# A one-core transform, gated block and expert kernel: VectorE's long steps cut up, column products put off, list scatters one at a time

## The chip, the cores and the metric

The kernel runs on one core of one Trainium2 chip. The metric is the device time of one execution in microseconds (us), the median of several runs. The engines are named as the profile names them: PE is TensorE's matmuls, DVE is VectorE, ACT is ScalarE, POOL is GpSimd and SP is SyncE, which issues most of the transfers.

## What is computed

There are three layers over 8 sequences of 3072 tokens with 256 channels, all in float32. The core of the reference:

```python
X = np.fft.rfft(x, axis=1)
Yr = shrink(Xr @ w_r - Xi @ w_i + b_r); Yi = shrink(Xr @ w_i + Xi @ w_r + b_i)   # soft threshold, 0.01
x = np.fft.irfft(Yr + 1j * Yi, n=3072, axis=1).reshape(24576, 256)
x = (sigmoid(x @ w_gate) * (x @ w_val)) @ w_out                                  # 256 -> 1536 -> 256
e = argmax(x @ moe2_gate); g = softmax(x @ moe2_gate)[e]                         # 8 experts
out = x + (x @ w_skip > 0) * g * (relu(x @ w1[e]) @ w2[e])                       # 256 -> 1024 -> 256
```

## The kernel before

To keep float32 accuracy on a float16 array, a matrix is stored as a high half and a low half, and each product is three matmuls (high-high, high-low, low-high). The high half comes from ACT and the low half from a subtraction on DVE or POOL, so every product waits for an ACT and then a DVE or POOL instruction. The power-of-two scale of a tile is the largest magnitude over all partitions; the maximum over partitions is a small matmul ("spread", line 188) that rides in a bank of the gated block.

**The main loop.** The gated block is 768 units: 8 batches of 8 chunks (384 tokens) of 12 slices of the 1536 channels (`moe_gen`, line 969). A unit u issues 12 matmuls of 384 columns for gate and value of its own slice (line 986), then 9 matmuls of 265 columns for the slice of unit u-2 (line 1028). Between the two lie, for each slice, a sigmoid on ACT (tile `sg`), the product of gate and value on DVE (tile `h`), the high half on ACT and the low half on DVE (both in tile `hh`). In DVE's program the low half of unit u comes after everything that was queued behind unit u's product.

**The background.** After each unit, `build` runs steps of five other jobs, written as Python generators whose `yield` ends a step: `attn` (the forward transform, mixing and half of the inverse of the next batch, `attn_gen`, line 496), `y` (the rest of the inverse, one chunk of 384 tokens at a time), `route` (expert choice and lists for a finished batch, `route`, line 1066), `prep` (expert weights) and `start`. The order of the instructions on each engine is the order in which the steps were issued, so the planner, not the hardware, decides what stands in front of what. A step's cost is estimated by a `Meter` (line 141): 0.07 us for each instruction plus its elements at the engine's rate; the cost of a step is the larger of VectorE plus GpSimd and ScalarE. A unit has room for 2.0 us (`BUDGET`), of which up to 0.3 (`CARRY`) is carried over; overdrawn room is carried as well. Jobs have due times in units, and of those that are due the one that is longest due goes first. `attn` is spread over a stretch of units in proportion to its steps' costs; `k.due` puts a single step off without moving that plan, so later steps run closer together until the plan is met. `route` has a step each 3.2 units (1.0 in the last batch). When `y` is due for a batch that `attn` has not finished (a few units after its planned end), it runs the rest of `attn` itself, and these steps count against no room.

**The places that the change touches.**

- Chunks of the forward transform (lines 656 to 676). Step by step for chunk c: load the input of chunk c+3 (SP); `cols`, 24 matmuls of 256 columns, and `evict`; `amax`; then settle the scale of chunk c+1 and write its high half on ACT (1024 elements), whose low half on DVE is put off to the head of the next step; then two steps that bound chunk c+3.
- Scales of a batch (lines 690 to 722). One step: the maximum over the batch comes back from its spread, ten operations on single columns follow, then the bias tile `bb` (five operations of 256 or 512 elements) and `bg` (512 elements). Four steps of 0.5 us (`WAITS`) that issue nothing follow before the first `freq`.
- Frequency groups (`freq`, `mix_pair`, `inv`; 13 groups a batch). The group's sum tile `sm` is split on POOL (tile `x`), ACT reuses the buffer for `com`, and POOL then adds `bg` to it (`yf`), on the way to the second mixing product.
- Routing's second step (lines 1086 to 1096): eleven DVE operations, on 192 elements for a whole batch (T = 24 tiles of 128 tokens) and on 24 for a chunk of the last batch (T = 3).
- The scatter of routed entries (lines 1126 to 1133): T indirect DMAs issued by POOL, three to a step.

Of the kernel before, what the change touches and what calls it, by code (L numbers as in the profile page):

```python
# [9 lines left out]
F32 = mybir.dt.float32  # L10
# [3 lines left out]
ALU = mybir.AluOpType  # L14
AX = mybir.AxisListType

NB, SEQ, D = 8, 3072, 256
N1, N2, NK, HN = 48, 64, 24, 32
NJ = 4
NC = HN // NJ  # L20
CT = 2 * N1 * NJ
NT3 = CT // 128
# [10 lines left out]
WAITS = 4  # L33
# [107 lines left out]
class Meter:  # L141
# [5 lines left out]
    def __getattr__(self, name):  # L147
        f = getattr(self.eng, name)

        def call(*a, **kw):  # L150
            self.sum += 0.07 + max(v.free_size() for v in a if hasattr(v, "free_size")) / self.rate
            return f(*a, **kw)  # L152

        return call
# [53 lines left out]
def absmax(k, out, in_, axis=AX.X):  # L208
    k.V.tensor_reduce(out, in_, axis=axis, op=ALU.max, apply_absolute_value=True)
# [286 lines left out]
def attn_gen(k, b):  # L496
    nc, V = k.nc, k.V
# [20 lines left out]
    def load(i):  # L518

        e, c = b + i // NC, i % NC  # L520
        if e < NB:
            xv = k.d.x[e].rearrange("(n h j) d -> h n j d", h=2, j=HN)
            x32[e, c] = k.xbuf[c % 4 if e == 0 else (e * NC + c) % 3]
            for h in range(2):
                nc.sync.dma_start(x32[e, c][h * 64:h * 64 + N1], xv[h, :, c * NJ:(c + 1) * NJ, :])

    def bound(c, h=None):
        if h is None:
            absmax(k, mx[:, 0, c:c + 1], x32[b, c], axis=AX.XY)
        else:  # L530
            absmax(k, (px if h else mx)[:, h, c:c + 1], x32[b, c][:, 2 * h:2 * h + 2], axis=AX.XY)
        if h == 1:
            V.tensor_tensor(mx[:, 0, c:c + 1], mx[:, 0, c:c + 1], px[:, 1, c:c + 1], op=ALU.max)
        if h == 1:
            tops[c] = allpow(k, px[:, 0, c:c + 1], mx[:, 0, c:c + 1], 2.0**-40)

    def scale(c):
        yield from settle(k, tops.pop(c))
        inv_pow2(k, px[:, 1, c:c + 1], px[:, 0, c:c + 1], 9)
# [35 lines left out]
    def amax(c):  # L575
        a_ = ah.pop(c).rearrange("p h j l e -> p (h j) l e")
        absmax(k, px[:, 2, c:c + 1], a_[:, :, 0], axis=AX.XY)
# [60 lines left out]
    if b == 0:  # L638
        for c in range(4):
            load(c)  # L640
        k.pace = 0.0
        yield
        k.pace = R1
        yield from first_cols()
    else:
        bg = k.gp.tile([128, 2, D], F32, tag="bg", name=f"bg_{b}", bufs=1)
        yield
        for c in range(3):
            bound(c, 0)
            yield  # L650
            bound(c, 1)
            yield
        yield from scale(0)
        halve(0)
        yield
        for c in range(NC):
            load(c + 3)
            yield
            cols(c, ((k.pa, "pa"),) * 2)
            evict(c, 0)  # L660
            evict(c, 1)
            yield
            if c > 0:
                amax(c - 1)
            yield
            if c + 1 < NC:
                yield from scale(c + 1)
                halve(c + 1)
            else:
                scales()  # L670
            yield
            if c + 3 < NC:
                bound(c + 3, 0)
                yield
                bound(c + 3, 1)
                yield
        yield 0.5
        amax(NC - 1)
    V.tensor_tensor(px[:, 2], px[:, 2], px[:, 0], op=ALU.mult)
    V.tensor_reduce(col(0), px[:, 2], axis=AX.X, op=ALU.max)  # L680
    top = allpow(k, col(3), col(0), 2.0**-60)
# [3 lines left out]
    def fetch(g):  # L685
        al = als[g] = k.wp.tile([128, 2, 2, D], F16, tag="al", name=f"al_{b}_{g}", bufs=AL)
        for i, k1 in enumerate(groups[g]):
            src = asc.rearrange("(r q) j l e -> q j r (l e)", r=4)[k1]
            nc.sync.dma_start(al[:, i].rearrange("p l e -> p (l e)"), src)

    for g in range(AL):
        fetch(g)
    yield
    if b:
        yield from settle(k, top)
    inv_pow2(k, col(4), col(3), 1)
# [4 lines left out]
    V.scalar_tensor_tensor(col(8), col(5), 2.0**-29, col(7), op0=ALU.mult, op1=ALU.mult)  # L701
    V.tensor_scalar(col(9), col(7), LAM, None, op0=ALU.mult)
    V.tensor_scalar(col(10), col(7), -LAM, None, op0=ALU.mult)
    bb = k.sp.tile([128, 2, D], F32, tag="bb", name=f"bb_{b}", bufs=1)
    for i in range(2):
        V.tensor_scalar(bb[:, i], k.bias[:, 0], k.chk[:, NC + i:NC + i + 1], None, op0=ALU.mult)
        V.scalar_tensor_tensor(
            bb[:, i], k.bias[:, 1], k.chk[:, NC + 2 + i:NC + 3 + i], bb[:, i], op0=ALU.mult, op1=ALU.add
        )
    if b:  # L710
        V.tensor_scalar(bb, bb, col(7), None, op0=ALU.mult)
    else:
        V.tensor_scalar(bb, bb, col(7), col(9), op0=ALU.mult, op1=ALU.add)
# [7 lines left out]
        V.tensor_scalar(col(14), col(10), 2.0, None, op0=ALU.mult)  # L721
    yield
    k.pace = 1.0
    for _ in range(WAITS):
        V.sum += 0.5
        yield

# [338 lines left out]
def route(k, b, t0, T):  # L1066

    nc, V, rp = k.nc, k.V, k.rp
    R = k.R[b][:, t0:t0 + T]
    L, S = R[:, :, 1:], R[:, :, 0]  # L1070
    tile_ = lambda tag, dt=F32, shape=None: rp.tile(shape or [128, T * NE], dt, tag=tag, name=f"{tag}_{b}_{t0}", bufs=1)
    tt = tile_("rt", shape=[128, 4, T])
    mx, sm, ac, gt = (tt[:, i] for i in range(4))
    et = lambda v: v.rearrange("p (e t) -> p e t", e=NE)
    te = lambda v: v.rearrange("p (e t) -> p t e", e=NE)
    bc = lambda v: v.unsqueeze(1).broadcast_to([128, NE, T])
    be = lambda v: v.unsqueeze(2).broadcast_to([128, NE, T])
    Le = L.rearrange("p t e -> p e t")
    dl, oh, w1, w2 = tile_("rdl"), tile_("roh"), tile_("rw1"), tile_("rw2")
    V.tensor_reduce(mx, L, axis=AX.X, op=ALU.max)  # L1080
    V.tensor_tensor(et(dl), Le, bc(mx), op=ALU.subtract)
    V.tensor_scalar(w1, dl, 0.0, None, op0=ALU.is_ge)
    k.S.activation(w2, dl, AF.Sigmoid)
    k.S.activation(dl, dl, AF.Sigmoid, scale=-1.0)
    yield
    V.reciprocal(dl, dl)
    V.tensor_tensor(dl, w2, dl, op=ALU.mult)
    V.tensor_tensor(et(w1), et(w1), be(k.rc[:, 0:NE]), op=ALU.mult)
    V.tensor_reduce(mx, te(w1), axis=AX.X, op=ALU.max)
    V.tensor_tensor(et(oh), et(w1), bc(mx), op=ALU.is_equal)  # L1090
    V.tensor_reduce(sm, te(dl), axis=AX.X, op=ALU.add)
    V.tensor_scalar(sm, sm, 1e-9, None, op0=ALU.add)
    V.reciprocal(gt, sm)
    V.tensor_scalar(ac, S, 0.0, None, op0=ALU.is_gt)
    oa = tile_("roa", F16)
    V.tensor_tensor(et(oa), et(oh), bc(ac), op=ALU.mult)
    yield
    ps = k.pa.tile([128, 512], F32, tag="pa", name="ps")
    W = T * NE
    nc.tensor.matmul(ps[:, :W], k.m16[:, 0], oa, start=True, stop=True)  # L1100
    nc.tensor.matmul(ps[:, W:2 * W], k.m16[:, 1], oa, start=True, stop=True)
    tot = tile_("rtot")
    V.tensor_copy(tot, ps[:, W:2 * W])
    V.tensor_tensor(w1, ps[:, :W], tot, op=ALU.subtract)
    yield
    V.memset(w2, 1.0)
    V.memset(et(w2)[:, :, 0:1], 0.0)
    V.tensor_tensor(et(tot)[:, :, 0], et(tot)[:, :, 0], k.base, op=ALU.add)
    inc = tile_("rdl")
    V.tensor_tensor_scan(inc, w2, tot, 0.0, op0=ALU.mult, op1=ALU.add)  # L1110
    V.tensor_copy(k.base, et(inc)[:, :, T - 1])
    yield
    V.tensor_tensor(w1, w1, inc, op=ALU.add)
    V.tensor_tensor(et(w1), et(w1), be(k.rc[:, NE:2 * NE]), op=ALU.add)
    V.tensor_tensor(w1, w1, oa, op=ALU.mult)
    V.tensor_reduce(sm, te(w1), axis=AX.X, op=ALU.add)
    yield
    V.tensor_scalar(ac, ac, -BIG, BIG, op0=ALU.mult, op1=ALU.add)
    idx = rp.tile([128, T], I32, tag="ridx", name="ridx", bufs=2)
    V.tensor_tensor(idx, sm, ac, op=ALU.add)  # L1120
    ent = rp.tile([128, T, 4], F32, tag="rent", name="rent", bufs=2)
    V.memset(ent[:, :, 3:4], 0.0)
    V.tensor_copy(ent[:, :, 0], gt)
    V.tensor_scalar(ent[:, :, 1:3], k.ids[:, t0:t0 + T, :], float(b * SEQ), None, op0=ALU.add)
    yield
    for t in range(T):
        if t % 3 == 0 and t:
            yield
        nc.gpsimd.indirect_dma_start(  # L1129
            out=k.lst, out_offset=bass.IndirectOffsetOnAxis(ap=idx[:, t:t + 1], axis=0),  # L1130
            in_=ent[:, t, :], in_offset=None, bounds_check=LROWS * BT - 1, oob_is_err=False,
        )
    yield
# [251 lines left out]

def build(tc, d, nb=NB, nstat=NSTAT, dbg=None):
    PSTEP = 3.9 * nb / NB
    BUDGET = 2.0
    CARRY = 0.3
    LEAD = 9  # L1390
    YSTEP = 0.9
    PRE = 2
# [9 lines left out]
    k = K()  # L1402
# [5 lines left out]
    with ExitStack() as top, tc.manual_schedule():  # L1408
# [166 lines left out]
        for _ in moe_gen(k, [(b, c) for b in range(nb) for c in range(NC)]):  # L1575
            room = min(room, CARRY) + BUDGET
            while room > 0:
# [94 lines left out]
```

## Time and profile before

| what | us |
|---|---|
| median of 3 runs (3607.19 to 3609.6) | 3607.56 |
| the profiled execution, its own time | 3600.82 |
| its span, first to last instruction | 3598.9 |

The profiled execution has a mean granted TensorE clock of 0.983. A line of a profile view names the line of the kernel, the engine, the operation and the tiles (out <- in). Where a helper records the operations, they all have line 152, and the tiles tell them apart. "Idle before" is the time for which the engine stood still before an instruction, and the name behind the arrow is what ended the wait. PEclk is the granted share of the clock: 1.0 is 2.4 GHz and 0.5 is 1.2 GHz.

### The profile page before, as it was taken

The page shows a single profiled execution, that of the slowest core. Times are in us where ns is not written, and L with a number is a line of the kernel's source. Part 1 is how long each engine was busy: PE and PEld are TensorE (multiplying, and loading weights), DVE is VectorE, ACT ScalarE, POOL GpSimd, SP SyncE. Part 2 cuts the span into 40 slices and gives each one's busy share as a digit, 9 for nine tenths or more (in the row PEclk, how much of TensorE's full clock was granted, in tenths as well). Part 3 has the DMA queues.
Part 4 walks back from the last instruction along what each step waited for, and adds up shares of the span by engine and source line. Part 5 has one row for each costly group of instructions (what it writes and reads, how often), then busy time and mean ns, then how long its engine had stood idle before and what let it go on. Part 6 is the DMA issues. An engine that isn't in the chain of part 4 may idle for free. (4 is left out here: it accounts for less than half of the span.)

```text
span 3598.9 us, 69199 instructions
## 1 busy us (share of the span) xinstructions
PE 3384.8 (94%) x26957; PEld 2379.7 (66%) x26958; DVE 2352.7 (65%) x5505; ACT 1664.2 (46%) x3276; POOL 698.3 (19%) x677
## 2 busy tenths in 40 slices
PE   4679999999999999999999999999999999999997
PEld 3456766676677666666766676667766666667675
DVE  7867677667776766666667676767645555665554
ACT  4545455455554544454445454544443343333332
POOL 3500100220031002200220022002200211333332
PEclk9889999999999999999999999999999999999999
DMA  6334233323322323232223231322211021444442
GB/s 167 116 101 120 75 96 93 90 70 97 103 82 75 110 72 89 69 97 86 81 72 96 80 102 57 97 75 81 84 42 37 28 86 51 149 145 144 163 155 102
DMA packets 230330, 336.07 MB, mean 93 GB/s; under 512 B 40705, under 2 KB 184835, under 8 KB 222736
## 3 DMA queue, kind: packets, MB, share of 16 engines
q1 hardware_dynamic: 213824, 305.31, 28.1%
q0 software_dynamic: 15744, 25.99, 2.4%
q8 instruction: 212, 3.47, 0.4%
q14 instruction: 118, 0.97, 0.1%
q10 hardware_dynamic: 432, 0.33, 0.0%
HBM read 177.86 MB, written 134.09 MB: 87 GB/s over the span
## 5 line engine op out<-in xcount | busy, mean ns | idle before, releaser
L986 PE MATMUL pg<-yT,wgv 128*128 128x384 f16 x9216 | 1654.7, 328 | 16.6 <-ACT sg L152 12.9
L986 PEld LDWEIGHTS <-wgv 128*128 128x128 f16 x9216 | 886.6, 98 | 565.8 <-issue 58.7
L1028 PE MATMUL pz<-wo,hh 128*128 128x265 f16 x6912 | 922.6, 278 | 26.8 <-DVE hh L152 22.7
L152 DVE TENSOR_TENSOR hh<-h,hh 128x384 f16<-128x384 f32 x768 | 447.8, 583 | 623.8 <-ACT hh L152 622.1
L1028 PEld LDWEIGHTS <-hh 128*128 128x128 f16 x6912 | 675.4, 98 | 225.6 <-DVE hh L152 31.3
L152 ACT ACTIVATE sg<-pg,ys 128x384 f32<-128x384 f32 x768 | 442.9, 577 | 570.8 <-PE pg L986 569.6
L152 DVE SCALAR_TENSOR_TENSOR h<-pg,sg 128x384 f32<-128x384 f32 x768 | 422.7, 550 | 5.3 <-PE pg L986 5.3
L152 ACT CAST hh<-h 128x384 f16<-128x384 f32 x768 | 387.0, 504 | 60.9 <-DVE h L152 60.6
L1129 POOL DMA_INDIRECT lst<-rent,ridx x192 | 197.1, 1027 | 573.7 <-DVE rent L152 310.2
L1374 PE MATMUL py<-we,h 128*128 128x256 f16 x2400 | 271.4, 273 | 1.4 <-DVE h L152 0.7
L1354 PE MATMUL ph<-zT,we 128*128 128x512 f16 (+3 forms) x1344 | 267.1, 356 | 5.6 <-DVE h L152 4.8
L152 POOL TENSOR_TENSOR ah<-tmp,ah 128x512 f16<-128x512 f32 x64 | 74.1, 1157 | 938.9 <-ACT ah L152 665.4
L1374 PEld LDWEIGHTS <-h 128*128 128x128 f16 x2400 | 233.3, 98 | 33.7 <-DVE h L152 1.6
L1354 PEld LDWEIGHTS <-we 128*128 128x128 f16 x1344 | 127.7, 98 | 135.4 <-issue 10.4
L152 POOL TENSOR_TENSOR x<-sm,x 128x256 f16<-128x256 f32 x77 | 56.1, 729 | 817.7 <-ACT x L152 614.7
L152 PEld LDWEIGHTS <-x 128*128 128x128 f16 x1842 | 182.2, 100 | 37.8 <-DVE sm L152 5.4
L152 ACT ACTIVATE h<-ph 128x512 f16<-128x512 f32 (+3 forms) x224 | 122.2, 548 | 183.7 <-PE ph L1354 181.5
L152 DVE SCALAR_TENSOR_TENSOR h<-ph,h 128x512 f16<-128x512 f32 (+3 forms) x224 | 141.1, 632 | 62.4 <-ACT h L152 60.8
L1380 POOL DMA_INDIRECT out_dram<-og,ix x100 | 99.4, 994 | 247.8 <-DVE gr L152 82.8
L152 DVE SCALAR_TENSOR_TENSOR og<-py,gr,zg 128x256 f32<-128x256 f32 x100 | 48.3, 483 | 141.6 <-PE py L1374 141.1
L1310 POOL DMA_INDIRECT zg<-zs,ix x100 | 102.3, 1023 | 131.3 <-DVE zh L152 38.4
L152 PE MATMUL ps<-wri,x 128*128 128x256 f16 x918 | 123.2, 281 | 4.5 <-ACT y L152 2.0
(236 smaller groups left out, 3391.1 us busy)
## 6 DMA issues: line engine op xcount, KB each, us to landing
we<-w SPq DMA_DIRECT2D x56, 1024.0 KB, 5.4
x<-in_x_dram SPq DMA_DIRECT2D x128, 192.0 KB, 3.5
asc<-ah SPq DMA_DIRECT2D x256, 96.0 KB, 2.0
al<-asc SPq DMA_DIRECT2D x192, 128.0 KB, 2.6
zsc<-zh SPq DMA_DIRECT2D x192, 128.0 KB, 2.1
zt<-zsc SPq DMA_DIRECT2D x64, 384.0 KB, 3.9
zs<-zo SPq DMA_DIRECT2D x64, 384.0 KB, 2.6
yh<-yn SPq DMA_DIRECT2D x308, 64.0 KB, 2.0
```

The source lines that it names most:

```text
L152: return f(*a, **kw)
L986: nc.tensor.matmul(ps[:, :CT], k.wgv[:, t, g, a, f * 128:(f + 1) * 128], yT[:, t, w, :], start=n == 0, stop=n == 5)
L1028: nc.tensor.matmul(zs[(b, c)][t][:, :ZW], hh[:, a, t * 128:(t + 1) * 128], k.wo[:, f, w, :], start=f == 0 and i == 0, stop=f == NF - 1 and ...
L1129: nc.gpsimd.indirect_dma_start(out=k.lst, out_offset=bass.IndirectOffsetOnAxis(ap=idx[:, t:t + 1], axis=0), in_=ent[:, t, :], in_offset=No ...
L1310: nc.gpsimd.indirect_dma_start(out=st.z[:, q, :], out_offset=None, in_=zs, in_offset=bass.IndirectOffsetOnAxis(ap=st.ix[:, 1, q:q + 1], ax ...
L1354: k.nc.tensor.matmul(ps, st.w[0][:, a, t * FE + f * 128:t * FE + (f + 1) * 128], st.zT[:, t, w, :], start=m == 0, stop=m == 5,)
L1374: k.nc.tensor.matmul(ps[:, :D], st.h[f][:, a, q * 128:(q + 1) * 128], st.w[1][:, w, f * D:(f + 1) * D], start=n == 0, stop=n == 23,)
L1380: k.nc.gpsimd.indirect_dma_start(out=k.d.out, out_offset=bass.IndirectOffsetOnAxis(ap=st.ix[:, 0, q:q + 1], axis=0), in_=o[:, q], in_offse ...
```

## The change

The meter charges 0.15 us for an instruction instead of 0.07, and a unit has room for 2.5 us with 0.4 carried instead of 2.0 with 0.3. In `attn_gen`, for all batches but the first, the step with a chunk's products may run no earlier than two units after the step that queued the chunk's low half. The last `amax` of a batch gets a step of its own; the bias tile is written ahead of the settling of the batch's scale, in two steps; the column operations are one step and the scaled bias tiles another; one empty step follows instead of four. Routing's second step is three steps where T is over 3. Scatters go one to a step in batches 0 to 5 and stay at three to a step in the last two.

```diff
@@ Meter
-            self.sum += 0.07 + max(v.free_size() for v in a if hasattr(v, "free_size")) / self.rate
+            self.sum += 0.15 + max(v.free_size() for v in a if hasattr(v, "free_size")) / self.rate
@@ attn_gen, chunks of batches 1 to 7
         for c in range(NC):
             load(c + 3)
+            k.due = k.unit + 2
             yield
             cols(c, ((k.pa, "pa"),) * 2)
             evict(c, 0)
...
         yield 0.5
         amax(NC - 1)
+        yield
     V.tensor_tensor(px[:, 2], px[:, 2], px[:, 0], op=ALU.mult)
...
     for g in range(AL):
         fetch(g)
     yield
+    bb = k.sp.tile([128, 2, D], F32, tag="bb", name=f"bb_{b}", bufs=1)
+    for i in range(2):
+        V.tensor_scalar(bb[:, i], k.bias[:, 0], k.chk[:, NC + i:NC + i + 1], None, op0=ALU.mult)
+        V.scalar_tensor_tensor(
+            bb[:, i], k.bias[:, 1], k.chk[:, NC + 2 + i:NC + 3 + i], bb[:, i], op0=ALU.mult, op1=ALU.add
+        )
+        if b:
+            yield
     if b:
         yield from settle(k, top)
     inv_pow2(k, col(4), col(3), 1)
...
     V.tensor_scalar(col(10), col(7), -LAM, None, op0=ALU.mult)
-    bb = k.sp.tile([128, 2, D], F32, tag="bb", name=f"bb_{b}", bufs=1)
-    for i in range(2):
-        V.tensor_scalar(bb[:, i], k.bias[:, 0], k.chk[:, NC + i:NC + i + 1], None, op0=ALU.mult)
-        V.scalar_tensor_tensor(
-            bb[:, i], k.bias[:, 1], k.chk[:, NC + 2 + i:NC + 3 + i], bb[:, i], op0=ALU.mult, op1=ALU.add
-        )
     if b:
+        yield
         V.tensor_scalar(bb, bb, col(7), None, op0=ALU.mult)
...
     k.pace = 1.0
-    for _ in range(WAITS):
+    for _ in range(1 if b else WAITS):
         V.sum += 0.5
         yield
@@ route
     V.reciprocal(dl, dl)
+    if T > NT3:
+        yield
     V.tensor_tensor(dl, w2, dl, op=ALU.mult)
     V.tensor_tensor(et(w1), et(w1), be(k.rc[:, 0:NE]), op=ALU.mult)
     V.tensor_reduce(mx, te(w1), axis=AX.X, op=ALU.max)
+    if T > NT3:
+        yield
     V.tensor_tensor(et(oh), et(w1), bc(mx), op=ALU.is_equal)
...
     for t in range(T):
-        if t % 3 == 0 and t:
+        if t and (b < NB - 2 or t % NT3 == 0):
             yield
         nc.gpsimd.indirect_dma_start(
@@ build
-    BUDGET = 2.0
-    CARRY = 0.3
+    BUDGET = 2.5
+    CARRY = 0.4
```

## Rows read from the trace of the kernel before

**Rows 1.** The page, part 1: busy time, share of the span, instructions.

```profile
PE 3384.8 (94%) x26957; PEld 2379.7 (66%) x26958; DVE 2352.7 (65%) x5505; ACT 1664.2 (46%) x3276; POOL 698.3 (19%) x677
```

**Rows 2.** Busy time in the main loop: length, engines, PEclk, DMA share, GB/s.

```profile
200.00:3020.00 2820.00, 2728.21 (x21965) 1915.61 (x21964) 1883.20 (x4388) 1375.06 (x2741) 419.60 (x404) 0.99 0.28 80
```

**Rows 3.** PE's waits from 200 to 3020: us in total, times, longest.

```profile
PE pz L1028 <- DVE hh L152: 22.7, 18, 2.2
PE ps L152 <- DVE xh L152: 20.7, 17, 3.1
PE pg L986 <- ACT sg L152: 12.9, 11, 3.7
...
PE ps L152 <- ACT xh L152: 4.6, 5, 1.6
```

**Rows 4.** Timeline, one inverse, one chunk's products: start, us, engine, instruction, [idle before].

```profile
820.74 0.38 PE L152 MATMUL ps<-yh,f 128*128 128x512 f16 x1 [2.83 <-DMA yh<-yn]
...
1273.03 1.15 ACT L152 ACTIVATE xh<-x,px 128x1024 f16<-128x1024 f32 x1 [2.85 <-DVE px L152]
...
1276.22 1.28 DVE L152 SCALAR_TENSOR_TENSOR xh<-x,px,xh 128x1024 f16<-128x1024 f32 x1
1277.55 1.28 PE L152 MATMUL ps<-xh,c 48*64 48x256 f16 x20 [3.01 <-DVE xh L152]
```

**Rows 5.** Stretches behind long waits of PE, columns as in rows 2.

```profile
1276.00:1284.00 8.00, 6.45 (x40) 3.68 (x40) 3.89 (x12) 3.21 (x6) 1.16 (x1) 0.57 0.37 98
...
2385.00:2390.00 5.00, 5.00 (x24) 2.93 (x25) 3.09 (x6) 2.12 (x4) 0.00 (x0) 0.66 0.16 52
...
1819.00:1824.00 5.00, 5.00 (x24) 2.64 (x22) 4.68 (x9) 2.43 (x6) 2.19 (x3) 0.66 0.17 55
...
820.00:825.00 5.00, 4.26 (x29) 2.86 (x30) 1.72 (x3) 1.69 (x4) 0.00 (x0) 1.00 0.74 248
```

**Rows 6.** Timeline at the scales of batch 2 (first line) and of batch 7.

```profile
640.07 0.40 PE L1028 MATMUL pz<-wo,hh 128*128 128x265 f16 x2 [1.44 <-DVE hh L152]
...
2379.16 0.55 DVE L152 SCALAR_TENSOR_TENSOR h<-pg,sg 128x384 f32<-128x384 f32 x1
...
2380.75 0.15 DVE L152 TENSOR_SCALAR bs<-bs 128x1 int32<-128x1 int32 x1
...
2384.38 0.55 DVE L152 TENSOR_TENSOR hh<-h,hh 128x384 f16<-128x384 f32 x1
...
2384.99 0.63 PE L1028 MATMUL pz<-wo,hh 128*128 128x265 f16 x4 [2.05 <-DVE hh L152]
```

**Rows 7.** Timeline at routing's second step, batches 0, 3 and 6.

```profile
609.74 0.40 PE L1028 MATMUL pz<-wo,hh 128*128 128x265 f16 x2 [1.26 <-DVE hh L152]
...
1692.84 1.34 DVE L152 RECIPROCAL rdl<-rdl 128x192 f32<-128x192 f32 x1
...
1698.20 0.36 DVE L152 TENSOR_TENSOR roa<-roh,rt 128x192 f16<-128x192 f32 x1
...
2754.02 0.29 PE L1028 MATMUL pz<-wo,hh 128*128 128x265 f16 x1 [2.24 <-DVE hh L152]
```

**Rows 8.** Timeline at scatters in front of a frequency group, three places.

```profile
690.49 0.48 PE L986 MATMUL pg<-yT,wgv 128*128 128x384 f16 x1 [2.80 <-ACT sg L152]
...
1815.52 0.97 POOL L1129 DMA_INDIRECT lst<-rent,ridx  x1 [1.37 <-DMA lst<-rent,ridx]
...
1817.23 0.47 ACT L152 ACTIVATE com<-ps,bs 128x256 f32<-128x256 f32 x1 [7.29 <-POOL x L152]
...
1818.22 1.14 PE L986 MATMUL pg<-yT,wgv 128*128 128x384 f16 x6 [3.73 <-ACT sg L152]
...
2179.21 0.32 PE L986 MATMUL pg<-yT,wgv 128*128 128x384 f16 x1 [1.25 <-ACT sg L152]
```

**Rows 9.** The products of batches 1 and 3: count, ns min/median/max, first and last start.

```profile
L152 PE MATMUL ps<-xh,c x192: 266/269/294, 225.5 to 309.4; 48*64 48x256 f16 x192
...
L152 PE MATMUL ps<-xh,c x192: 266/269/293, 845.8 to 944.8; 48*64 48x256 f16 x192
```

## The prediction

> **What bounds the kernel now.** I read the page's engine shares first: PE is busy for 94% of the span, VectorE for 65%, nothing else comes near [rows 1]. So a microsecond is won only where PE stands still or runs at the low clock. The second view cuts the span: in the main loop, 200 to 3020 us, PE is busy for 2728 of 2820 us, and the mean granted clock is 0.99 [rows 2]. That leaves 92 us of standing still, and about 28 us of clock (0.01 of 2820). The third view says what ended the waits of that stretch [rows 3]: low halves of the gated block (`hh`) 22.7 us in 18 waits, low halves of the transform's input (`xh`) 20.7 us in 17 and their high halves 4.6 us in 5, sigmoids (`sg`) 12.9 us in 11. Then I looked at the timeline where the long ones lie, and at the clock behind them. The unit's length is 2820 / 768 = 3.67 us.
>
> The start (to 200 us) and the expert blocks (from 3020 us) hold nothing that the change moves much: batch 0 keeps its steps apart from the bias tile's place, and T = 3 in the last batch's routing. I take both as unchanged.
>
> **The products behind the halves.** At 1273.03 ACT writes a chunk's high half, 1.15 us. VectorE's low half stands at the head of the next step and starts at 1276.22, behind the gated block's work, for 1.28 us. PE has the 24 matmuls in its program by then and waits 3.01 us for it [rows 4]. With two units, 7.3 us, between the step that queues the low half and the products, both have long ended: all of 20.7 + 4.6 = 25.3 us goes [rows 3]. Five of these waits have a fall of the clock to 1.2 GHz behind them, two of them like the one from 1276 with 0.57 over 8 us, three with 0.66 over 5 us, as the other falls are [rows 5]. Half rate for 0.86 of 8 us, some 6.9 us, of which 1 us was the wait itself, costs 3 us; half rate for 0.68 of 5 us, 3.4 us, costs at most 1.7, less the wait's tail 1.5. Together 2 x 3 + 3 x 1.5 = 10 us. **Term: -35.**
>
> What the wait delays: evictions, `amax` and the next chunk's scale come after it in the same generator; nothing else of the five jobs waits, and on the engines nothing stands in a queue, because the wait is in the planner. The load of chunk c+3 keeps its place ahead of it on SP. The price is lateness. The chunks of batch 1 lie (309.4 - 225.5) / 7 = 12 us or 3.3 units apart, those of batch 3 14.1 us or 3.9 units [rows 9]. Two units now pass idle for `attn`; the rest of a chunk needs about two more (the low half alone 1.28 us, and as much again for `amax` and the two bounds, which are as many elements). So batch 1 falls behind by 0.7 of a unit a chunk, five to six units in eight chunks, the others by almost nothing. Its frequency groups have the larger room to catch up; what is not caught up is run by `y` in a heap. Bounds: 0 if it catches up, 15 us if three groups are run one behind the other with PE standing for their chains. I take **+5**, nearer to 0, as the new room is a quarter larger.
>
> **A batch's scales.** In batch 7, VectorE has from 2380.75 to 2384.38, 3.6 us, of column operations and bias tiles ahead of the low half that PE wants; PE waits 2.05 us [rows 6]. From the end of the gated product (2379.71) to that low half 4.67 us pass, and the wait is 2.05, so some 2.6 us of background behind one product cost nothing. The new pieces are 0.8 us (one bias tile), again 0.8, about 1.5 (columns) and 1.3 us; any one fits, and two as well. Six of the 18 waits for `hh` stand behind this step, 1.44 the first and 2.05 the last, 9.9 us by my count. Three have a clock fall behind them like that of batch 7 from 2385 [rows 5], 1.7 us each. 9.9 + 5.1. **Term: -15.** The bias tile moves ahead of the settling of the scale; only the first and last frequency group of a batch read it, ten units later, and the last reader of the batch before is done. No instruction is added; the empty steps that go are paid by the new steps' own spacing.
>
> **Routing's second step.** From 1692.84 to 1698.56 VectorE works for it, 5.7 us, some of it held up by POOL's operations. Six of the 18 waits stand behind this step, 1.26 the first and 2.24 the last [rows 7], 9.4 us by my count, three with a clock fall. The pieces are 1.3, 1.3 and 1.9 us and lie 3.2 units apart. 9.4 + 5.1. **Term: -14.** The chunk-wise routing of the last batch keeps its step.
>
> **Scatters.** A scatter takes 0.97 us of POOL and waits for the landing of the one before, 1.37 us, so three hold POOL for over 7 us; ACT's `com` waits 7.29 us behind them, the sigmoid behind it on ACT, and PE 3.73 us for that [rows 8]. Three such places: 2.80 + 3.73 + 1.25 = 7.8 us; two clock falls add 2.6. A single scatter finds its forerunner landed, and holds `com` for 1 us. The place with a hold of 7.29 cost 3.73, so some 3.5 us are free. **Term: -10.** The work stays 192 scatters, but a batch's list takes 24 steps of 3.2 units instead of 8, with the other steps just over the 96 units of a batch; the lists of batches 1 to 5 so start late by some units each, and catch up in the last batch, where steps come each unit. The expert tables are needed only near unit 732, so I cost it at nothing; the cover is those units.
>
> **Meter and room.** The meter's 0.15 us is what a single-column operation takes [rows 6]. Costs of a 512-element step rise by an eighth, of small ones by double, the room by a quarter: a unit may get more, up to 2.9 us and the last step's overhang. That is over the 2.6 us that cost nothing. Six short waits for `hh`, 3.4 us in all, already come from such heaps. Bounds: -3 if they go, +45 if one unit in ten gets 0.6 us too much. I take **+10**, nearer to the row.
>
> **Sum.** -35 - 15 - 14 - 10 + 5 + 10 = -59 against the profiled execution's own 3600.8 us: 3542. The median of the runs shown is 6.7 us above that execution, so I forecast 3548 for a median.
>
> **The clock, row and rule.** The clock's part of the sum is 10 + 5 + 5 + 2.6 = 23 us. The rows tie falls to these waits: 0.66 from 2385, behind the wait of 2.05 us at 2384.99, yet 1.00 at 820, around a wait of 2.83 us [rows 4 to 6]. So a wait of two or three microseconds may cost the clock or not. The Trainium skill, page "TensorE: Matmul & The Clock Gate", Part 1, says that the gate falls back only after a whole idle window and that the window runs freely. By that rule waits this short would not lower the clock, the 23 us would stay lost, and the sum would be -36. The rows show falls behind them, so I keep the 23 us; the free-running window fits that not each wait has one.
>
> **Rivals.**
>
> 1. *The bursts move* (0.17). `attn` runs in heaps after each wait, the room is larger, and VectorE's blocks of over 2.6 us come elsewhere. For it: 40 of the 92 us of standing still lie at no step that the change touches, so heaps arise anywhere. Against it: VectorE stands idle for a third of the loop, 937 us [rows 2]. With the upper bound's 45 in place of 10: 3583.
> 2. *The clock stays* (0.04). The clock's falls have other causes, and only the waits go: 3548 + 23 = 3571. (It is the page's rule above; the rows at 2385 and 1276 speak against it.)
> 3. *Lateness* (0.11), slower. The two units a chunk are not caught up, in the other batches neither, because their plan leaves 3.9 units a chunk and y, lists and weights take their share. Then `y` comes due first and runs the rest of the transforms outside the room; PE stands for the chains of three groups, 15 us a batch. It decides from four batches on: four cost what I expect to gain, all seven 105 us, in place of my 5: 3648.
> 4. *It changes nothing* (0.08). With another meter every step lands elsewhere, and as many coincidences come as go: 3607.
>
> **How the numbers follow.** The forecast has 0.60. Its own range is 3515 (the four terms' 74 us whole, nothing given back, and half of the other 40 us of waits) to 3575 (the four terms at little over half). What a measurement of this kernel can tell from no change is about 0.2%, 7 us. Faster: 0.60 + 0.17 + 0.04 = 0.81; same 0.08; slower 0.11. The range 3515 to 3600 holds the forecast and rivals 1 and 2 and leaves out 3 and 4.
>
> **What the profile after would show.** Right: no wait of `ps` for `xh`, and products some 7 us behind the low half; no `hh` wait of over 1 us at scales and routing; scatters never two within 5 us before unit 672; main loop shorter by some 60 us, clock of the loop over 0.995. Wrong: many waits for `hh` and `sg` at new places (rival 1), a mass of transform steps at a batch's end with PE waiting for `yh`, `x` and `com` (rival 3), or PE's idle time gone and the clock as before (rival 2).

## The result and the profile after

The changed kernel takes 3550.67 us in the median of 4 runs (3547.05 to 3552.99) beside 3607.69 us for the kernel before: a ratio of 0.9847, 95% interval 0.9834 to 0.986. That is 57 us less. The forecast was 3548, range 3515 to 3600. The profiled execution took 3547.05 us with a span of 3545.1, 53.8 less than before.

First the main loop: its row beside [rows 2], then the waits of PE beside [rows 3] (who waits for whom: us in total, times, longest).

```profile
200.00:2955.00 2755.00, 2702.30 (x21968) 1907.90 (x21967) 1878.19 (x4360) 1378.19 (x2741) 426.62 (x401) 1.00 0.29 82
```

```profile
PE pg L188 <- DVE pp L152: 10.2, 5, 7.1
PE pg L188 <- ACT sg L152: 8.9, 10, 1.6
PE ps L152 <- DMA yh<-yn: 8.4, 3, 4.0
PE pz L1033 <- DVE R L152: 6.0, 9, 1.4
PE ps L152 <- DVE sm L152: 4.8, 6, 1.2
PE pg L991 <- ACT sg L152: 3.8, 6, 1.2
PE pz L1033 <- DVE hh L152: 3.6, 8, 0.6
```

PE stands still for 2755.0 - 2702.3 = 53 us instead of 92, and the loop's clock is 1.00 to two places instead of 0.99. Waits for `xh` are not among the rows any more; those for `hh` fell from 22.7 us to 3.6, none over 0.6 us; those of the gate's matmuls for `sg` from 12.9 to 3.8. But the waits for `pp` (the spread of a largest magnitude) grew from 1.8 us to 10.2, and those for `yh` from 3.9 to 8.4.

The timelines show each part where it works. A chunk's halves and products, beside [rows 4]:

```profile
1204.79 1.15 ACT L152 ACTIVATE xh<-x,px 128x1024 f16<-128x1024 f32 x1 [1.34 <-DVE px L152]
1205.97 1.28 DVE L152 SCALAR_TENSOR_TENSOR xh<-x,px,xh 128x1024 f16<-128x1024 f32 x1 [1.22 <-ACT xh L152]
...
1216.10 0.85 PE L152 MATMUL ps<-xh,c 48*64 48x256 f16 x24
```

The low half ends at 1207.25, and the 24 products run 8.9 us later in one piece. The scales of batch 7, beside [rows 6]:

```profile
2336.67 0.15 DVE L152 TENSOR_SCALAR bs<-bs 128x1 int32<-128x1 int32 x1
...
2338.22 0.47 DVE L152 TENSOR_SCALAR bg<-bias,bs 128x512 f32<-128x512 f32 x1
...
2338.61 0.55 DVE L152 TENSOR_TENSOR hh<-h,hh 128x384 f16<-128x384 f32 x1
...
2339.71 0.51 PE L1033 MATMUL pz<-wo,hh 128*128 128x265 f16 x3
```

The columns and the scaled bias tiles came to lie in one unit after all. Without the bias tile's own operations they are 1.9 us instead of 3.6, and PE does not wait. ACT's waits for POOL in front of `com`, first before and then after (the scatters' place, [rows 8]):

```profile
ACT com L152 <- POOL x L152: 80.6, 62, 7.3
```

```profile
ACT com L152 <- POOL x L152: 55.5, 62, 1.4
```

The longest fell from 7.3 to 1.4 us. One sign that I had named did not come: before unit 672, 63 scatters still start within 5 us of the one before (109 before the change, counted in the traces). A step gives a scatter its place in POOL's program only; when POOL stands still, as here for `com`, those queued behind run in a row:

```profile
800.18 1.26 POOL L152 TENSOR_TENSOR yf<-bg,com 128x512 f32<-128x512 f32 x1 [7.61 <-ACT com L152]
...
806.50 0.97 POOL L1138 DMA_INDIRECT lst<-rent,ridx  x1 [1.39 <-DMA lst<-rent,ridx]
```

A look at both spans shows a second thing. The gated products run from first to last start (count, ns min/median/max, stretch), before and after:

```profile
L152 DVE SCALAR_TENSOR_TENSOR h<-pg,sg x768: 542/551/558, 201.6 to 3027.8; 128x384 f32<-128x384 f32 x192
```

```profile
L152 DVE SCALAR_TENSOR_TENSOR h<-pg,sg x768: 541/550/556, 201.5 to 2961.9; 128x384 f32<-128x384 f32 x192
```

The loop is 2760.4 us long instead of 2826.2, **65.8 us** shorter, which is more than the whole gain. The expert stage behind it lasts 583 us instead of 571 and took 12 us back; the last section shows what is left over for it. "Loop" below is this length, of one profiled execution each; the executions of one kernel differ by 3 to 14 us.

### The profile page after: what moved, and what is told of

The parts are those of the page before. It is cut to its first block, busy times and chain, and to the rows that moved or that the text cites. A ratio compares the mean times of both kernels' runs of the same rounds, so it can differ in the third digit from the quotient of the medians.

```text
span 3545.1 us, 69209 instructions
## 1 busy us (share of the span) xinstructions
PE 3358.6 (95%) x26957; PEld 2370.2 (67%) x26958; DVE 2347.6 (66%) x5505; ACT 1666.9 (47%) x3276; POOL 708.7 (20%) x677
## 5 line engine op out<-in xcount | busy, mean ns | idle before, releaser
L1033 PE MATMUL pz<-wo,hh 128*128 128x265 f16 x6912 | 917.4, 277 | 10.2 <-DVE R L152 6.0
L1138 POOL DMA_INDIRECT lst<-rent,ridx x192 | 207.9, 1083 | 502.8 <-DVE rent L152 260.6
L152 POOL TENSOR_TENSOR yf<-bg,com 128x512 f32<-128x512 f32 x77 | 98.4, 1277 | 118.5 <-ACT com L152 118.5
```

The source lines that it names most:

```text
L1033: nc.tensor.matmul(zs[(b, c)][t][:, :ZW], hh[:, a, t * 128:(t + 1) * 128], k.wo[:, f, w, :], start=f == 0 and i == 0, stop=f == NF - 1 and ...
L1138: nc.gpsimd.indirect_dma_start(out=k.lst, out_offset=bass.IndirectOffsetOnAxis(ap=idx[:, t:t + 1], axis=0), in_=ent[:, t, :], in_offset=No ...
```

## The experiments

Theory A: each part takes away the waits at its own place. Rival B: the larger room and the truer meter did it, by moving every step; the cuts are interchangeable. Ratios are to the kernel before in the same set of runs; differences in us are differences of ratios times 3600. With the intervals given, such a difference is uncertain by some 8 us.

### Each part undone alone

For `undo_products`:

```diff
-            k.due = k.unit + 2
             yield
             cols(c, ((k.pa, "pa"),) * 2)
```

> The changed kernel (3551 us) without the two units' wait: a chunk's products may follow its low half at once again. Theory A (each part takes away the waits that stand at its own place): the 25 us of waits for the halves of the input and their 10 us of clock come back, and the 5 us of batch 1's lateness go, so about 3581, with PE waits for xh of 15 us or more in the main loop. Rival B (the larger room and the truer meter did it by moving every step; the single cuts are interchangeable): within 7 us of 3551.

For `undo_scales`, the old text of lines 678 to 726 of the kernel before (the diff shows the main hunks; the bias tile returns to its old place, and the step behind the last `amax` goes):

```diff
-        if b:
-            yield
...
     if b:
-        yield
         V.tensor_scalar(bb, bb, col(7), None, op0=ALU.mult)
...
-    for _ in range(1 if b else WAITS):
+    for _ in range(WAITS):
```

> The changed kernel with the batch's scales in one step again, four empty steps behind it. Theory A: PE waits of 1.4 to 2.2 us for hh behind that step in most of the seven batches and some falls of the clock, 15 us in all: about 3566. Rival B: within 7 us of 3551.

For `undo_routing` the two `if T > NT3: yield` go:

> The changed kernel with routing's second step in one piece again. Theory A: waits for hh of 1 to 2.2 us at up to seven places and some falls of the clock, 14 us in all: about 3565. Rival B: within 7 us of 3551.

For `undo_scatters`:

```diff
-        if t and (b < NB - 2 or t % NT3 == 0):
+        if t % 3 == 0 and t:
```

> The changed kernel with scatters three to a step in all batches again. Theory A: two or three waits of 1 to 4 us of PE for sg behind com, 10 us with the clock: about 3561. Rival B: within 7 us of 3551. A third way (rival C, single scatters are in the way of more transforms than three in a heap are): 3545 or less.

Measured:

| undone | ratio (95%) | worse than the change by, us | loop | loop longer by, us | forecast term |
|---|---|---|---|---|---|
| nothing | 0.9847 (0.9834 to 0.986) | | 2760.4 | | |
| products | 0.9917 (0.990 to 0.9933) | 25 | 2787.6 | 27.2 | 35 - 5 |
| scales | 0.9889 (0.9873 to 0.9906) | 15 | 2774.9 | 14.5 | 15 |
| routing | 0.9852 (0.9836 to 0.9869) | 2 | 2769.1 | 8.7 | 14 |
| scatters | 0.9858 (0.9841 to 0.9874) | 4 | 2773.9 | 13.5 | 10 |

PE's waits in the loop, one row or two of each kernel, and for the last three the longest at its place. Products undone:

```profile
PE ps L152 <- DVE xh L152: 19.4, 18, 3.0
...
PE ps L152 <- ACT xh L152: 4.2, 5, 2.0
```

Scales undone:

```profile
PE pz L1029 <- DVE hh L152: 11.3, 12, 2.3
```

```profile
1996.36 0.48 DVE L152 TENSOR_SCALAR bg<-bias,bs 128x512 f32<-128x512 f32 x1
...
1997.36 0.86 PE L1029 MATMUL pz<-wo,hh 128*128 128x265 f16 x6 [2.32 <-DVE hh L152]
```

Routing undone:

```profile
PE pz L1033 <- DVE hh L152: 12.4, 15, 2.3
...
PE ps L152 <- DMA yh<-yn: 1.8, 2, 1.1
```

```profile
1354.64 0.36 DVE L152 TENSOR_TENSOR roa<-roh,rt 128x192 f16<-128x192 f32 x1
...
1355.52 0.74 PE L1033 MATMUL pz<-wo,hh 128*128 128x265 f16 x5 [2.33 <-DVE hh L152]
```

Scatters undone:

```profile
PE pg L991 <- ACT sg L152: 10.8, 11, 2.3
```

```profile
2498.32 0.47 ACT L152 ACTIVATE com<-ps,bs 128x256 f32<-128x256 f32 x1 [4.75 <-POOL x L152]
...
2499.31 0.48 PE L991 MATMUL pg<-yT,wgv 128*128 128x384 f16 x2 [2.31 <-ACT sg L152]
```

Each wait comes back where theory A puts it: 23.6 us for `xh` (0 before the undoing), 11.3 and 12.4 us for `hh` (3.6), 10.8 us for `sg` (3.8). The totals also hold waits at other places, so I looked where the long ones lie: four of 1.5 to 2.3 us stand behind the scales, six of 0.7 to 2.3 behind routing, three of 1.5 to 2.3 behind `com`. Rival B says that none should, and it falls for products and scales by the time as well. For routing and scatters the time alone is what rival B said (2 and 4 us, under 7), and for routing it rules out my 14. Rival C falls: with the old scatters the ratio is not lower. Two things hide the two cuts. With routing undone, the waits for `yh` are also 6.6 us less (8.4 to 1.8), for a reason that was not tried. And in both kernels the expert stage is as short as before the change, 572 and 570 us, with less of the routing left over for it (last section); so they lose in the loop and win behind it.

### Meter and room

`undo_meter` takes back the meter, the room and the carry; `only_meter` makes that change alone in the kernel before; `only_products` makes only the two units' wait there.

```diff
-            self.sum += 0.15 + ...
+            self.sum += 0.07 + ...
-    BUDGET = 2.5
-    CARRY = 0.4
+    BUDGET = 2.0
+    CARRY = 0.3
```

> The changed kernel with the old meter (0.07 us an instruction) and the old room (2.0, 0.3 carried). Theory A, with the forecast's term of +10 for larger heaps: the four cuts alone give about 3541. Rival B (meter and room did it): 3590 or more. Rival D (the smaller room cannot make up for the chunks' two units, so the transforms end late and are run in a heap): 3565 or more, with PE waits for yh, com and x at the ends of batches 1 to 3.

> The kernel before with the new meter and room alone. Theory A: heaps cost 10 us more, about 3618. Rival B: 3570 or less.

> The kernel before (3608 us) with the two units' wait alone. Theory A: the waits for xh and their clock go, 35 us, less 5 for lateness: about 3578. Rival D: the old room cannot make up the two units, 3595 or more. Rival B: within 7 us of 3608.

Measured: `undo_meter` 0.9789 (0.9772 to 0.9805), 21 us faster than the whole change, loop 2748.6. `only_meter` 0.9953 (0.9937 to 0.997), 17 us faster than before. `only_products` 0.9928 (0.9907 to 0.9949), 26 us faster than before.

So rival B falls: the four cuts without meter and room gain 76 us, more than with them. Theory A's direction holds in `undo_meter`. Its term of 10 us was half of what is lost: 12 us lie in the loop, the other 11 in the expert stage (583 against 572 us). On the kernel before, though, meter and room alone gained 17 us where I expected a loss of 10; the waits for `hh` and `xh` there are 19.6 and 18.0 us, little under [rows 3]. PE stands still 11 us less in its loop than before, and the mean clock of its executions is 0.984 to 0.987 beside 0.982 to 0.986. That part of the expectation was wrong, and what won there is not settled. `only_products` wins nearly what its undoing loses (26 and 25), so this part does not lean on the others, and rival D (the old room cannot make up the two units) falls.

Rival D has a true core all the same. The waits of `undo_meter`, and the longest one in the timeline:

```profile
PE pg L188 <- ACT sg L152: 15.3, 16, 2.0
PE pg L991 <- ACT yT L152: 7.7, 2, 5.7
...
PE ps L152 <- DMA zt<-zsc: 3.0, 1, 3.0
PE pg L991 <- DVE yT L152: 2.9, 2, 2.3
```

```profile
524.18 0.48 PE L991 MATMUL pg<-yT,wgv 128*128 128x384 f16 x1 [5.75 <-ACT yT L152]
```

PE waits 13.6 us for chunks of the first batch's own inverse (`yT`, `zt`). As I read it, the transforms of batch 1, late by their two units, are served first, and `y` is late instead of them. That the two units bring this with the old room, `only_products` shows too: 4.9 + 4.8 us for `yT` and 4.4 for `zt`, 14.1 in all, where the kernel before has none. Everywhere else `undo_meter` is the calmest kernel so far.

### Meter or room, and a version without lateness

`room_only` has the old meter and the new room; `early_room` the old meter, the old room and 2.3 us in the first 96 units; `early_room_due` also one unit's wait instead of two in batch 1.

```diff
-            room = min(room, CARRY) + BUDGET
+            room = min(room, CARRY) + (BUDGET if u >= NU else 2.3)
```

> The changed kernel with the old meter (0.07 us) but the new room (2.5, 0.4 carried). With the old room too, the ratio to the kernel before was 0.979, with both new 0.985. Theory F (the room's heaps cost the difference: with the old meter the same room lets still more into a unit, but batch 1 is not late): 0.982 to 0.988, with PE's waits in many small pieces in all batches. Rival G (the dearer meter costs it, by putting steps off): 0.976 or less.

> The four cuts with the old meter and the old room of 2.0, but room 2.3 in the first 96 units. With the old room throughout (ratio 0.979), PE waited 13.6 us for chunks that the lagging inverse delivered late near 470 and 524 us, with falls of the clock behind it. Theory H (lateness in the first batch is what the two units cost, and a little more room there pays it): those waits go, 15 to 20 us, ratio 0.974 to 0.976. Rival F (any larger room gives as much back in heaps): 0.978 or more.

> As early_room, and in batch 1 the products wait for one unit instead of two. Theory H: batch 1 is less late still, nothing more is to be had from it, and some waits for xh return: within 5 us of early_room. Rival I (lateness still costs there): 5 us or more faster than early_room.

| kernel | meter, room | ratio (95%) | loop |
|---|---|---|---|
| the change | 0.15, 2.5 | 0.9847 (0.9834 to 0.986) | 2760.4 |
| `undo_meter` | 0.07, 2.0 | 0.9789 (0.9772 to 0.9805) | 2748.6 |
| `room_only` | 0.07, 2.5 | 0.9882 (0.9866 to 0.9899) | 2776.9 |
| `early_room` | 0.07, 2.3 then 2.0 | **0.976 (0.9744 to 0.9776)** | 2738.9 |
| `early_room_due` | the same | 0.9773 (0.9757 to 0.979) | 2741.1 |

With the old meter the larger room costs 0.9882 - 0.9789 = 33 us. The dearer meter takes a part of that back; that it does so by filling the same room with less work is my reading, and the dearer meter with the old room was not run. The first two rows of the waits of `room_only`:

```profile
PE pg L991 <- ACT sg L152: 20.9, 36, 1.9
PE pg L188 <- DVE pp L152: 16.8, 15, 1.9
```

These are many and short, none over 2 us, which is what theory F says of heaps of steps in one unit. PE stands still for 68 us in this loop against 40 in that of `undo_meter`, yet the mean clock of the span is 0.991 against 0.987, and no stretch of the loop is below full clock. Rival G falls. `early_room` is the fastest: 0.976 of the time before, and 31 us under the change. Its waits for `yT` and `zt` are gone from the rows; its list begins with

```profile
PE pg L188 <- ACT sg L152: 10.0, 11, 1.6
PE ps L152 <- DMA yh<-yn: 6.5, 4, 3.3
```

One unit for batch 1 wins nothing more (0.9773; the intervals overlap), as theory H expected. The same edit in all batches was tried on the change itself:

```diff
-            k.due = k.unit + 2
+            k.due = k.unit + 1
```

> The changed kernel with one unit instead of two between the low half and the products. Theory A: one unit (3.7 us) covers the low half where VectorE is less than half a unit behind, so up to half of the 25 us of xh waits return, while batch 1 is less late (5 us): 3551 to 3565. Rival E (the wait is needed only so that the two steps don't share a unit): 3551 or less, no xh waits over 1 us.

It gave 0.9865 (0.9849 to 0.9882), loop 2766.5. That lies within what theory A allowed and is not told apart from the change. Waits for `xh` are 4.8 us, none over 1.0: one unit covers nearly all low halves too, which is the sign that rival E named. So theory A and rival E stay undecided here.

### Routing and scatters where few other waits are left

`early_room_old_lists` is `early_room` with the edits of `undo_routing` and `undo_scatters`.

> early_room (ratio 0.976, about 3516 us beside 3600) with routing's second step in one piece and scatters three to a step again: what these two cuts are worth where few other waits are left. Theory A, with the forecast's terms of 14 and 10: ratio 0.981 to 0.984, with waits of 1 to 2.3 us for hh behind routing and of 1 to 4 us for sg behind com. Rival J (what undoing each alone showed, 2 and 4 us: other work covers them): 0.9785 or less.

Measured: 0.9868 (0.9851 to 0.9884), 39 us slower than `early_room`, loop 2775.7 against 2738.9. The waits, and two of them in the timeline:

```profile
PE pz L1033 <- DVE hh L152: 13.6, 13, 3.4
PE pg L991 <- ACT sg L152: 13.3, 10, 5.0
...
PE ps L152 <- ACT com L152: 6.4, 5, 2.4
```

```profile
603.72 0.40 PE L1033 MATMUL pz<-wo,hh 128*128 128x265 f16 x2 [3.35 <-DVE hh L152]
...
1091.15 0.48 PE L991 MATMUL pg<-yT,wgv 128*128 128x384 f16 x1 [5.00 <-ACT sg L152]
```

Rival J falls: in this kernel no other work covers the two cuts. The first wait stands behind routing's second step, the second behind a `com` that scatters held. They are worth 39 us here, more than the 24 of the forecast. How the 39 divide between the two was not tried.

## Why the prediction was right

The time, 3550.67, is 3 us from the forecast, and the mechanism holds: long steps in front of a low half or a sigmoid were what PE stood still for. By its steps:

- **Products, -35 + 5.** 25 us by undoing and 26 alone, 30 forecast. The waits that came back, 23.6 us, are the 25.3 of [rows 3] nearly whole. The clock behind them was not over-sized: of the 27 us of loop, 13 are PE standing still (65.6 against 52.7 us) and 14 are PE busy for longer (2722.0 against 2707.7 us), at a mean clock of the span of 0.985 against 0.989; I had 10. The lateness was under-sized: with the wait undone, waits for `pp` fall from 10.2 to 0.8 us and those for `R` from 6.0 to 1.2. The lag itself is there as worked out: batch 1's products run from 231.1 to 330.6, 14.2 us or 3.9 units a chunk (I had said about 4) against 3.3 [rows 9].

```profile
L152 PE MATMUL ps<-xh,c x192: 269/269/294, 231.1 to 330.6; 48*64 48x256 f16 x192
```

- **Scales, -15.** 15 measured by undoing.
- **Routing and scatters, -14 and -10.** Under-sized together: 39 us in a kernel with few other waits. In the changed kernel itself each undone alone showed 2 and 4 us, but 8.7 and 13.5 us of loop.
- **Meter and room, +10.** 21 us by undoing, but 12 of them in the loop, where the term was meant. I had priced heaps by waits for `hh` alone; those are short. Beside `undo_meter`, the changed kernel has more waits for `pp` (10.2 against 1.6 us) and `yh` (8.4 against 1.2), and in `room_only` it is `sg` and `pp`. Nor had I seen that the room was needed at the start only, where `y` is late.
- **Expert blocks unchanged, late lists at nothing.** This step failed, by 12 us in the profiled execution: the loop gave 65.8 us where I had 59, and the expert stage took 12 back. I had taken it that the lists catch up within the last batch. They do not, and what is left of them runs between the expert products. That the total is only 3 us off is luck: these two errors cancel.
- **The rivals.** Heaps (1) happened and cost what the meter's row above says, not all of 45. Lateness (3) shows as 13.6 and 14.1 us in the two kernels with the old room, at the start alone, and decides nothing; the lateness that costs is that of the lists. That nothing changes (4) fell.
- **The clock (2).** The mean clock of the whole span went from 0.983 to 0.989: 0.017 x 3599 - 0.011 x 3545 = 22 us of clock, against 23 in the sum. Other executions of the kernel before had 0.982 to 0.986, so this is uncertain by some 7 us. In the loop the trace has 15 falls to 1.2 GHz before and 3 after.

So the falls went with the waits, as the rows had it. The Trainium skill, "TensorE: Matmul & The Clock Gate", Part 1, read as I had read it (short waits leave the clock alone), would have left it at 0.983; the measurement decides. That a window runs freely would fit that not each wait has a fall (the 2.83 us wait of [rows 4] is at full clock in [rows 5]); no run here tests it.

## What to carry to other kernels

In a program ordered by a planner, look for the longest single step in front of what the bound engine needs, and cut it or move it off; undoing a cut brings its waits back at that very place, which tests the reading better than the total does. Put a product off by a unit or two from the step that makes its input, but look who is served later because of it, and pay there alone: the larger room and dearer meter for all units gave back 21 of the 76 us that the cuts had won. A job that is spread thinner ends later; look where its rest then runs.

## What the runs showed that was not expected

The expert stage lasts between 570 and 583 us in the profiled executions. The change edits nothing in it, but the planner runs there what is left of the lists, between the expert products. Each list has one product of `roa` (line 1100, then 1109); in this stage, before and after:

```profile
L1100 PE MATMUL ps<-roa,m x1: 173/173/173, 3036.3 to 3036.3; 128*128 128x24 f16 x1
```

```profile
L1109 PE MATMUL ps<-roa,m x2: 176/176/177, 2967.7 to 3002.6; 128*128 128x24 f16 x2
```

One chunk's list is left before, two after: the scatters of batch 6 run in units 701 to 720 instead of 683 to 702, and those of the last batch's chunks come late behind them. The first 40 us of the stage, columns as in [rows 2], before and after:

```profile
3028.00:3068.00 40.00, 37.78 (x254) 23.46 (x251) 26.37 (x87) 15.22 (x31) 11.90 (x12) 1.00 0.35 111
```

```profile
2962.00:3002.00 40.00, 35.87 (x230) 21.74 (x228) 25.34 (x87) 14.72 (x31) 9.89 (x10) 0.96 0.32 105
```

PE comes 24 matmuls less far in them, with a wait of 3.1 us for `roa` and a fall of the clock. Two lists are left in four of the fourteen kernels: the changed one, those with products or scales undone, and `due_one`, which alone have the dearer meter, the routing in three steps and the single scatters together. Their stages last 577 to 583 us, those of the other ten 570 to 578. The 289th product of `ph` starts 143 to 145 us into the stage in the four and at 136 to 139 in the ten. Against the kernel before that is 145 against 137, so about 8 of the 12 us are lost in the first quarter of the stage, where the second list is made; the rest stays open. PE's waits in the stage, in the changed kernel and then with routing undone:

```profile
PE ph L1363 <- DVE h L152: 8.8, 8, 2.5
PE py L1383 <- issue: 4.0, 7, 0.9
PE ps L1109 <- DVE roa L152: 3.1, 1, 3.1
```

```profile
PE ph L1359 <- DVE h L152: 5.7, 6, 2.4
PE ps L1105 <- DVE roa L152: 0.6, 1, 0.6
```

15.9 us against 6.3 and some shorter ones. The waits marked `issue` end on nothing that the profile shows, and their cause stays open.

The longest new wait, 7.1 us, is none of the change's own steps: VectorE stood 8.76 us in front of the first look at an expert's weights, whose transfer had not landed, and the spread of a chunk behind it was late.

```profile
528.83 0.69 DVE L152 TENSOR_REDUCE psc<-pw 128x1 f32<-128x512 f32 x1 [8.76 <-DMA pw<-in_moe_w_dram]
...
530.81 0.29 PE L188 MATMUL pg<-idb,pp 128*128 128x128 bf16 x1 [7.09 <-DVE pp L152]
```

A step on an engine that works in order, moved ahead of its transfer, stops everything behind it. In `undo_meter` and `early_room` no wait for `pp` is longer than 1.2 us, and with products undone none is over 0.8; with scales, routing or scatters undone the longest is 6.3 to 6.5. So it goes with the two units and the dearer meter together.
